# Block-sparse attention with a gated projection on one core: output weights staged in other buffers, projections gated on the value weights alone, new order tables

## The chip, the cores and the metric

One core of a Trainium2 chip runs the whole program in one launch. The metric is device time in microseconds (us) from one execution; lower is better. The engines are TensorE (PE, with its weight loads shown as PEld), VectorE (DVE), ScalarE (ACT), GpSimd (POOL) and SyncE (SP, which here only issues transfers).

## The reference

Attention over 4 batches, 8 heads, 768 positions, head size 64, in blocks of 32. A query block sees its own block and the two beside it, the first and the last block, and three drawn blocks; the first and the last query block see all. The attention output, written as rows of 512, then goes through a gated projection:

```python
scores = np.where(mask, scale * np.matmul(q, k.transpose(0, 1, 3, 2)), -1000000000.0)
attn = softmax(scores)                       # over the seen keys
x = np.matmul(attn, v)                       # -> (4, 768, 512)
for k in range(5):                           # causal convolution along the rows
    gate_pre += conv_w[k][None, None, :] * xp[:, k:k + S, :]
gate = 1.0 / (1.0 + np.exp(-gate_pre))
out = (gate * (x @ w_val)) @ w_out           # w_val, w_out: 512 x 512
```

## The kernel before, in words

The unit of attention work is a pair of neighbouring query blocks (11 pairs in a batch) or half of the first-and-last query blocks (two units in a batch), 52 units in all. The main loop runs one step for each unit n, and in a step it writes, for each engine, the work of several units that are in different states: the scores of unit n (`sc`, or `s` for the first-and-last blocks), the products with the values of unit n-2 (`av`), the turning of the probabilities of unit n-1 (`pt`), and the turning of the attention rows of unit n-3 (`xp`) into `xT`. The other engines serve these: DVE takes the row maxima (`mx`) and normalizes (`rs`, `x`); ACT takes the exponentials (`pe`, or `rest` and `first`), copies the turned probabilities from PSUM (`ptr`), copies `xT` and scales the queries (`qc`); POOL gathers the value rows of drawn blocks by an indirect transfer (`vb`) and copies drawn key blocks (`kg`). Which engine copies which key block, scales the queries of which batch, and so on is set by strings of letters at the head of the file (`KEYS_BY`, `OWN_BY`, `Q_ON`, `NEAR`). Each engine executes its instructions in the order in which they were written.

Beside attention runs the gated projection. A batch's rows are two tiles of 384. For a tile, `gates` makes the gate (ACT `th` and DVE `th`, 16 DVE passes of 128x384), `split` writes `xT` as a rounded part `xh` (four ACT passes) and a rest `xl` (four POOL passes), and `project` multiplies with the value weights (`vp`, 48 matmuls), evicts the gated values (`y`, `yh`, `yl`) and multiplies with the output weights (`op`, 36 matmuls). How many pieces of `project` and of the preparation stand at which half step is set by the digits in `FILLS` and `STEPS`.

The weights arrive as 64-bit words in eight chunks of 512 KB (four of `w_val`, then four of `w_out`), each into a staging buffer `wst`. Four decode passes on DVE (`words`, `wst`, `wst`, `words`), a cast on ACT (`wv` or `wo`) and a subtraction on POOL or DVE turn a chunk into a rounded part and a rest. Before the change all eight chunks are staged in the buffers of `xh`, `xl`, `yh` and `yl`, four at a time, so `split` may begin only when the last four are staged and two of them are decoded, and `project` only when all eight are decoded.

Of the kernel before, what the change touches and what calls it, by code (L numbers as in the profile page):

```python
# [20 lines left out]
DM = H * D  # L21
# [9 lines left out]
V_AT = ((0, 3, 7), (1, 4, 8), (0, 1, 4), (1, 3, 8))  # L31
K_AT = ((9, 10, 11), (11, 11, 11), (2, 11, 11), (1, 4, 4))
LAG_T, LAG_V, LAG_X = 1, 2, 3
WEIGHTS_AT = (0, 1, 6, 7, 8, 10, 12, 15)
# [7 lines left out]
    "PPAAAAPPPAAAPPPAAAPPPAAAPPPAAAPPPAAAPPPAAAPPPAAAPPPAAAPPPAAAPPAAAA",  # L42
    "AAAPPPPAASSSPPPSSSPPPPAAPPPSSSPPPVVVPPPSSSPPPSSSPPPSSSSSSSSSPPPSSS",
    "SSSSSSSSSSSSPSSSSSPPPPPSPPSSSSPPSSSSPSVVVVPSSSSSPPSSSSPSSSSSPSSSSS",
    "PASSSSPASSSSSSAAAAPASSSSAVSSSSPASSSSPASSSSSSSSSAPAASSSVVVVVVPASSSS",
)
NEAR = (
    "GGGGGGCCGGGGGCGCGGGGGG",
    "GGGGGGGGGGGGGGGGGGGGGG",
    "GGGGGGGGGCGGGGGGGGCGGG",  # L50
    "GGGGGGGGGCCGGGGGGGCGCG",
)
Q_ON = "AAVV"
OWN_BY = (
    "DPDPDPDPDVDPDPDPVPDPDP",
    "DPDPDPPPDPDPDPAPPPVPDA",
    "ADADADADADADADAAADADAD",
    "PPPPPPPPDPPPPPPPPVPPPP",
# [4 lines left out]
XT_ON = "VVAAAAAAAAAAAVAAAAAAAAAAVAAAAAAAAAAAAAAAAAAVVAVAVAVA"  # L63
GATHER = "WUGGGGGGGUGSSSSUSUGSGUSGSSGGGSSGGGGGGGGGGGSGGGGGGGGGGUUU"

BULK_BY = "SSSSSASSSSSSSSSASSSSSSSSSSSSSSSS"
# [8 lines left out]
    "11200001313200100202234322"  # L75
    "00020031021101112223041301"
    "21011101111121012110010202"
    "11011021212101010101050101"
    "213030"
)  # L80
STEPS = (
    "20111015213401132202221312"
    "21304021020202020314440534"
    "02311340003240051012082142"
    "23320113212020102130402231"
    "000012"
# [5 lines left out]
def attention_moe(ctx, tc, qb, kb, v, ve, sampled, w_val, conv_w, w_out, ident_in, slot_in, out):  # L92
# [148 lines left out]
    staged = []  # L241

# [4 lines left out]
    def load_weights():  # L247

        for n in range(2 * CH):
            st = const.tile([128, CH, TS], F32R, tag=("xh", "xl", "yh", "yl")[n % 4], name="wst")  # L250
            flat = st.bitcast(I32).rearrange("p c n -> p (c n)")[:, 0 : 2 * DM]
            c = n % CH
            queue(24 + n).dma_start(flat, (w_val if n < CH else w_out).bitcast(I32)[c * 128 : (c + 1) * 128, :])
            staged.append((step[0], flat.rearrange("p (n w) -> p n w", w=2)))
            yield
# [514 lines left out]
    def queue_rows(bt, t):  # L770
        m = Rows()
        m.bt, (m.t, m.n), m.ready, m.begun = bt, TILES[bt.b][t], [], False
# [11 lines left out]
    def fill(times=1):  # L784
        for _ in range(times):
            if set(range(2 * CH)) <= decoded and to_project and step[0] > max(to_project[0][0].ready):
                begun.add("project")
                advance(to_project)
# [168 lines left out]
```

## Time and profile before

| | |
|---|---|
| median of 3 runs | 365.35 us (364.81 to 367.18) |
| the profiled execution, whole | 366.3 us |
| its span, first to last instruction | 364.4 us |
| PE busy | 346.8 us, 95% of the span |
| DVE, ACT, POOL busy | 268.2, 249.4, 219.0 us |
| mean granted TensorE clock | 0.984 |

The profiled execution lies 0.95 us above the median, and 1.9 us of it lie outside the span. In the profile's rows an engine's idle time stands in brackets with what ended it; `[0.66 <-ACT ptr L110]` means that the engine stood for 0.66 us until ACT's write of `ptr`. All instructions go through one recording helper, so their line is L110 in all rows, and they are told apart by their tiles. Times are from the span's start.

### The profile page before, as it was taken

Reading aid. Unit: us, or ns where it says so; the run is one execution under the profiler, and the core shown is the slowest. Engines: PE = TensorE matmul, PEld = TensorE weight load, DVE = VectorE, ACT = ScalarE, POOL = GpSimd, SP = SyncE. Lnnn points to the kernel's source line nnn. Section 1 sums busy time; section 2 is a strip of 40 time slices with the busy share of each in tenths; the row PEclk is TensorE's granted clock in tenths of the full one; section 3 lists DMA queues with packets and bytes.
Section 4 is the critical chain, followed back from the end, with each engine's and each line's share of the span. In section 5 each row is a group of like instructions: output and inputs, shape, how many; then the busy total and the mean of one; then the engine's idle time right before and its main releaser. Section 6 shows DMA issues by size and latency. Waiting matters only on the chain.

```text
span 364.4 us, 14299 instructions
## 1 busy us (share of the span) xinstructions
PE 346.8 (95%) x5650; PEld 273.0 (75%) x5650; DVE 268.2 (74%) x616; ACT 249.4 (68%) x613; POOL 219.0 (60%) x327
## 2 busy tenths in 40 slices
PE   8698999997999999999999999999999999999995
PEld 7265576664676977787689787986798778989894
DVE  3559769978798788885988588966957878485930
ACT  2678799998798576777695776975655867645431
POOL 1775758799885585776653684566537544525440
PEclk9689999999999999999999999999999999999999
DMA  6997996999559985975457289776432244110202
GB/s 218 309 349 209 303 271 207 297 309 290 152 166 310 265 251 160 293 225 151 116 163 246 70 246 269 212 223 205 120 109 89 77 150 147 31 58 31 86 2 87
DMA packets 44644, 68.08 MB, mean 187 GB/s; under 512 B 6081, under 2 KB 26945, under 8 KB 44577
## 3 DMA queue, kind: packets, MB, share of 16 engines
q1 hardware_dynamic: 36704, 43.09, 39.1%
q0 software_dynamic: 6880, 22.77, 20.9%
q10 hardware_dynamic: 992, 1.30, 1.2%
q8 instruction: 45, 0.74, 0.8%
q14 instruction: 23, 0.18, 0.2%
HBM read 60.84 MB, written 6.29 MB: 184 GB/s over the span
## 4 chain that ended last, share of the span: by engine, by line
PE 63%; ACT 5%; DVE 3%; POOL 1%; issue 1%; ACTq 0%; DVEq 0%
PE vp L110 18%; PE op L110 17%; PE av L110 10%; PE pt L110 8%; PE sc L110 7%; PE xp L110 2%; PE s L110 1%; ACT ptr L110 1%; ACT pe L110 1%; DVE qc L110 1%; ACT th L110 1%; POOL yl L110 1%; POOL vb L110 1%; DVE mx L110 1%; ACT ot L110 0%
## 5 line engine op out<-in xcount | busy, mean ns | idle before, releaser
L110 POOL DMA_INDIRECT vb<-in_v,idx x88 | 88.5, 1006 | 71.1 <-PE av L110 46.4
L110 ACT ACTIVATE pe<-sc,mx 128x256 f32<-128x256 f32 x176 | 69.3, 485 | 36.9 <-DVE mx L110 36.7
L110 DVE SCALAR_TENSOR_TENSOR th<-xT,cw,th 128x384 f32<-128x384 f32 x128 | 89.0, 706 | 4.6 <-ACT th L110 2.3
L110 DVE TENSOR_REDUCE mx<-sc 128x2 f32<-128x512 f32 x88 | 56.6, 684 | 24.1 <-PE sc L110 23.9
L110 ACT COPY ptr<-pt 128x512 f32<-128x512 f32 x103 | 59.9, 610 | 4.4 <-PE pt L110 4.3
L110 POOL COPY kg<-k 128x128 f32 (+1 forms) x163 | 56.9, 387 | 9.5 <-DMA k<-in_k 9.1
L110 PE MATMUL sc<-kg,qc 64*32 64x256 f32 x1408 | 57.5, 399 | 5.3 <-POOL kg L110 3.2
L110 POOL TENSOR_TENSOR yl<-y,yh 128x384 fp32r<-128x384 f32 x32 | 32.5, 1021 | 38.6 <-ACT yh L110 36.4
L110 PE MATMUL op<-wo,yh 128*128 128x512 f32 x192 | 53.7, 401 | 0.0
L110 PE MATMUL vp<-xh,wv 128*128 128x384 f32 x256 | 51.4, 343 | 0.0
L110 PE MATMUL pt<-ident,pe 128*128 128x128 f32 x352 | 50.9, 283 | 0.0
L110 PEld LDWEIGHTS av<-va,ptr 128*32 128x32 f32 (+1 forms) x1056 | 30.9, 118 | 24.3 <-ACT ptr L110 13.1
L110 PE MATMUL av<-va,ptr 128*32 128x65 f32 (+1 forms) x1056 | 40.4, 226 | 4.4 <-ACT ptr L110 3.4
L110 PEld LDWEIGHTS vp<-xh,wv 128*128 128x128 f32 x256 | 43.9, 188 | 0.2
L110 PEld LDWEIGHTS pt<-ident,pe 128*128 128x128 f32 x352 | 39.1, 142 | 5.8 <-issue 0.8
L110 PEld LDWEIGHTS sc<-kg,qc 64*32 64x32 f32 x1408 | 24.9, 109 | 24.4 <-issue 8.8
L110 POOL TENSOR_TENSOR xl<-xT,xh 128x384 fp32r<-128x384 f32 x32 | 33.4, 1050 | 11.3 <-ACT xh L110 11.3
L110 PEld LDWEIGHTS op<-wo,yh 128*128 128x128 f32 x192 | 35.0, 188 | 7.0
L110 PE MATMUL av<-vb,ptr 128*32 128x65 f32 x1408 | 38.3, 222 | 1.8 <-DMA vb<-in_v,idx 1.6
L110 PEld LDWEIGHTS av<-vb,ptr 128*32 128x32 f32 x1408 | 30.3, 110 | 4.0 <-DMA vb<-in_v,idx 2.1
L110 PE MATMUL op<-wo,yl 128*128 128x512 f32 x96 | 31.9, 412 | 0.2 <-POOL yl L110 0.2
L110 DVE SCALAR_TENSOR_TENSOR y<-th,vp 128x384 f32<-128x384 f32 x32 | 17.6, 550 | 19.2 <-PE vp L110 16.3
(74 smaller groups left out, 470.9 us busy)
## 6 DMA issues: line engine op xcount, KB each, us to landing
kg<-in_k SPq DMA_DIRECT2D x111, 64.0 KB
qc<-in_q SPq DMA_DIRECT2D x48, 128.0 KB
out<-ot SPq DMA_DIRECT2D x23, 256.0 KB
vn<-in_v SPq DMA_DIRECT2D x11, 520.0 KB
va<-in_v SPq DMA_DIRECT2D x44, 130.0 KB
k<-in_k SPq DMA_DIRECT2D x11, 512.0 KB
wst<-in_w_val SPq DMA_DIRECT2D x4, 512.0 KB
wst<-in_w_out SPq DMA_DIRECT2D x4, 512.0 KB
```

The costliest lines, as they stand in the source:

```text
L110: made = getattr(self.eng, name)(*args, **kwargs)
```

## The change: what it does

The four value chunks stay in the buffers of `xh`, `xl`, `yh` and `yl`. Three of the four output chunks go into one buffer of `xT`, the one that the second batch's turned rows use later, and the fourth into a gate buffer `th`. `split` needs only the first two value chunks to be decoded; `project` needs only the value weights for its first four pieces and all weights for the rest. All the tables at the head of the file are written anew.

```diff
-V_AT = ((0, 3, 7), (1, 4, 8), (0, 1, 4), (1, 3, 8))
-K_AT = ((9, 10, 11), (11, 11, 11), (2, 11, 11), (1, 4, 4))
+V_AT = ((1, 3, 7), (3, 3, 6), (1, 1, 6), (0, 3, 5))
+K_AT = ((9, 11, 11), (11, 11, 11), (3, 9, 10), (1, 3, 4))
-WEIGHTS_AT = (0, 1, 6, 7, 8, 10, 12, 15)
+WEIGHTS_AT = (0, 0, 6, 6, 7, 10, 11, 15)
...
-    "AAAPPPPAASSSPPPSSSPPPPAAPPPSSSPPPVVVPPPSSSPPPSSSPPPSSSSSSSSSPPPSSS",
+    "SSSSAAAAAAAASSSAAAPPPPAAPPPSSSSSSAAAPPPSSSPPPSSSPPPSSSPPPSSSPPPPSS",
...
-Q_ON = "AAVV"
+Q_ON = "AAVA"
...
     staged = []
+    wide_room = two.tile([128, CH, KW - 1 + S], F32, tag="xT", name="wst")
...
         for n in range(2 * CH):
-            st = const.tile([128, CH, TS], F32R, tag=("xh", "xl", "yh", "yl")[n % 4], name="wst")
-            flat = st.bitcast(I32).rearrange("p c n -> p (c n)")[:, 0 : 2 * DM]
+            if n < CH:
+                st = const.tile([128, CH, TS], F32R, tag=("xh", "xl", "yh", "yl")[n], name="wst")
+            elif n == 2 * CH - 1:
+                st = two.tile([128, CH, TS], F32, tag="th", name="wst")
+            else:
+                st = wide_room
+            first = 2 * DM * (n - CH) if CH <= n < 2 * CH - 1 else 0
+            flat = st.bitcast(I32).rearrange("p c n -> p (c n)")[:, first : first + 2 * DM]
...
     def fill(times=1):
         for _ in range(times):
-            if set(range(2 * CH)) <= decoded and to_project and step[0] > max(to_project[0][0].ready):
+            if not to_project or step[0] <= max(to_project[0][0].ready):
+                return
+            m = to_project[0][0]
+            if set(range(CH if m.groups < CH else 2 * CH)) <= decoded:
                 begun.add("project")
+                m.groups += 1
                 advance(to_project)
...
-        if {CH, CH + 1} <= decoded and len(staged) == 2 * CH and to_split and unread <= {id(to_split[0][0])}:
+        if {0, 1} <= decoded and to_split and unread <= {id(to_split[0][0])}:
             advance(to_split, prepared)
...
-        if k < 2 * CH and n >= WEIGHTS_AT[k] and (k < 4 or k - 4 in decoded):
+        if k < 2 * CH and n >= WEIGHTS_AT[k]:
             next(weights)
```

What the tables do shows in the order of the engines' instructions. On PE the first `vp` keeps its place: in both kernels it is row 582 of PE's order, in step 23, and the order of kinds of matmuls around it is the same. What moves is the work of the other engines.

On ACT, in steps 11 and 12 of the loop before the change, from the copies of the turned halves (`ptr`) of step 11 on:

```order
L110 COPY ptr<-pt 128x512 x2
L110 CAST wo_156<-words 128x512
L110 COPY xT<-xp 128x4x64
L110 ACTIVATE qc<-qc 128x256
L110 ACTIVATE pe<-sc,mx 128x256 x4
```

On ACT, in the same place of step 11 now:

```order
L110 COPY ptr<-pt 128x512
L110 CAST xh<-xT 128x384
L110 COPY ptr<-pt 128x512
L110 CAST wo_156<-words 128x512
L110 CAST xh<-xT 128x384
L110 COPY xT<-xp 128x4x64
```

Two of the four `xh` casts of the first tile stand in step 11 now, one of them between the two `ptr` copies; the other two follow in step 12, behind six copies of drawn key blocks (`kg` 128x128) where two stood.

On ACT, in step 15 before the change, where the first two casts stood:

```order
L110 COPY ptr<-pt 128x512
L110 CAST wo_156<-words 128x512
L110 CAST xh<-xT 128x384
L110 COPY ptr<-pt 128x512
L110 CAST xh<-xT 128x384
```

On ACT, in step 15 now:

```order
L110 COPY ptr<-pt 128x512 x2
L110 CAST wo_156<-words 128x512
L110 ACTIVATE th<-xT,cw 128x384
L110 COPY xT<-xp 128x4x64
L110 ACTIVATE qc<-qc 128x256
```

Both turned halves are copied ahead of the cast of the output weights, which stood between them. In step 14 a gate's first pass (`th`) stood between the two copies, and stands in step 15 now; a `wo` cast went from step 13 to step 14.

On POOL, from the value weights' subtraction of step 11 on, now (before, `wv` was followed by the `vb` row at once, the four `xl` stood in steps 15 to 17, and step 12 had one `kg` copy of a drawn block more, step 13 three more):

```order
L110 TENSOR_TENSOR wv_155<-words,wv_154 128x512
L110 TENSOR_TENSOR xl<-xT,xh 128x384
L110 DMA vb<-in_v,idx 128x520 x2
L110 COPY kg_147<-k 128x256
L110 COPY kg_147<-k 128x2x128
L110 TENSOR_TENSOR wo_157<-words,wo_156 128x512
L110 TENSOR_TENSOR xl<-xT,xh 128x384 x2
L110 DMA vb<-in_v,idx 128x520 x2
```

The subtractions `xl`, each of which needs ACT's `xh`, stand ahead of the value gathers `vb` of the next step now.

Further moves: the drawn key blocks of step 10 are one fewer on ACT, those of step 11 one fewer, those of step 13 three more. In step 18 three drawn key blocks went from DVE, where they stood between the row maxima and the decode passes of the last weight chunk, to ACT. The scaling of the fourth batch's queries (`qc`) left DVE for ACT as a whole. The third chunk of output weights is loaded a step earlier; the steps in which the chunks are decoded stay the same but for one.

## Rows read from the trace of the kernel before

**Rows 1.** The page's first part: busy time, share of the span, instructions.

```profile
PE 346.8 (95%) x5650; PEld 273.0 (75%) x5650; DVE 268.2 (74%) x616; ACT 249.4 (68%) x613; POOL 219.0 (60%) x327
```

**Rows 2.** Stretches: length, then busy PE, PEld, DVE, ACT, POOL, clock, DMA.

```profile
60.67:77.22 16.55, 15.73 (x362) 11.43 (x361) 15.39 (x36) 16.05 (x46) 13.29 (x22) 1.00 0.98 289
77.22:119.31 42.09, 37.89 (x783) 27.24 (x783) 34.70 (x85) 35.88 (x90) 33.22 (x58) 1.00 0.79 237
119.31:240.00 120.69, 120.26 (x2074) 97.87 (x2072) 98.40 (x214) 84.12 (x203) 74.81 (x105) 1.00 0.70 206
```

**Rows 3.** The chain that ended last: start, length, what.

```profile
108.66 1.17 PE av L110 x44
...
137.39 1.02 PE sc L110 x32
138.41 1.21 PE av L110 x48
139.62 1.02 PE pt L110 x8
...
142.05 0.22 PE xp L110 x2
```

**Rows 4.** PE in order of time: start, length, what, idle before and its end.

```profile
79.97 0.57 PE L110 MATMUL av<-va,ptr 128*64 128x65 f32 x12 [0.66 <-ACT ptr L110]
...
84.97 0.57 PE L110 MATMUL av<-va,ptr 128*64 128x65 f32 x12 [1.30 <-ACT ptr L110]
...
91.01 0.66 PE L110 MATMUL av<-vb,ptr 128*32 128x65 f32 x30 [1.22 <-DMA vb<-in_v,idx]
...
119.31 1.64 PE L110 MATMUL vp<-xh,wv 128*128 128x384 f32 x8
```

**Rows 5.** ACT in order of time, steps 11, 15 and 18.

```profile
65.16 1.01 ACT L110 COPY kg<-k 128x128 f32 x4
66.07 1.06 ACT L110 COPY ptr<-pt 128x512 f32<-128x512 f32 x2
67.13 0.62 ACT L110 CAST wo<-words 128x512 fp32r<-128x512 f32 x1
67.66 0.36 ACT L110 COPY xT<-xp 128x256 f32<-128x256 f32 x1
...
83.40 0.62 ACT L110 CAST wo<-words 128x512 fp32r<-128x512 f32 x1 [0.96 <-DVE words L110]
83.93 0.51 ACT L110 CAST xh<-xT 128x384 fp32r<-128x384 f32 x1
84.34 0.58 ACT L110 COPY ptr<-pt 128x512 f32<-128x512 f32 x1
...
100.53 0.62 ACT L110 CAST wo<-words 128x512 fp32r<-128x512 f32 x1 [1.39 <-DVE words L110]
```

**Rows 6.** POOL in order of time, steps 13 and 15.

```profile
72.14 0.99 POOL L110 DMA_INDIRECT vb<-in_v,idx  x1 [2.02 <-PE av L110]
...
83.81 0.94 POOL L110 DMA_INDIRECT vb<-in_v,idx  x1 [0.30 <-issue]
...
86.01 0.99 POOL L110 TENSOR_TENSOR xl<-xT,xh 128x384 fp32r<-128x384 f32 x1
```

**Rows 7.** DVE in order of time, step 18.

```profile
97.47 0.29 DVE L110 TENSOR_SCALAR_CACHE_REDUCE kg<-k 128x128 f32 x1 [0.87 <-issue]
...
98.34 0.16 DVE L110 TENSOR_SCALAR rs<-av 128x4 f32<-128x4 f32 x1
```

**Rows 8.** Two scalings of queries on DVE, in order of time.

```profile
259.93 0.29 DVE L110 TENSOR_SCALAR qc<-qc 128x256 f32<-128x256 f32 x1
276.38 4.17 DVE L110 TENSOR_SCALAR qc<-qc 128x256 f32<-128x256 f32 x1
```

**Rows 9.** The stretch around the longer one, columns as in rows 2.

```profile
275.00:280.00 5.00, 5.00 (x96) 3.87 (x94) 4.09 (x2) 2.49 (x6) 5.00 (x7) 1.00 0.34 102
```

**Rows 10.** PE in order of time, behind that stretch.

```profile
284.78 0.34 PE L110 MATMUL av<-va,ptr 128*32 128x65 f32 x8 [0.63 <-ACT ptr L110]
```

More of the change, by code (lines that the diff above doesn't have):

```diff
@@ L41 @@
 KEYS_BY = (
-    "PPAAAAPPPAAAPPPAAAPPPAAAPPPAAAPPPAAAPPPAAAPPPAAAPPPAAAPPPAAAPPAAAA",
-    "AAAPPPPAASSSPPPSSSPPPPAAPPPSSSPPPVVVPPPSSSPPPSSSPPPSSSSSSSSSPPPSSS",
-    "SSSSSSSSSSSSPSSSSSPPPPPSPPSSSSPPSSSSPSVVVVPSSSSSPPSSSSPSSSSSPSSSSS",
-    "PASSSSPASSSSSSAAAAPASSSSAVSSSSPASSSSPASSSSSSSSSAPAASSSVVVVVVPASSSS",
+    "PPAAAAPPPAAAPPPAAAPPPAAAPPPPAAPPPAAAPPPAAAPPPAAAPPPAAAPPPAAAPPPAAA",
+    "SSSSAAAAAAAASSSAAAPPPPAAPPPSSSSSSAAAPPPSSSPPPSSSPPPSSSPPPSSSPPPPSS",
+    "SSSSSSPPSSSSSSSSSSPPPPPSPPPSSSPSSSSSPSVVVVPSSSSSPPSSSSPSSSSSPSSSSS",
+    "PASSSSPASSSSSSAAAAPASSSSAVSSSSPASSSSPASSSSPASSSSPAASSSVVVVVVPASSSS",
 )
 NEAR = (
-    "GGGGGGCCGGGGGCGCGGGGGG",
+    "GGGGGGCCGGGGCCCCGCGCGG",
     "GGGGGGGGGGGGGGGGGGGGGG",
-    "GGGGGGGGGCGGGGGGGGCGGG",
-    "GGGGGGGGGCCGGGGGGGCGCG",
+    "GGCGGGGGGCGGGGGGGGCGGG",
+    "GGGGGGGGGGGGGGGGGGCGCG",
 )
-Q_ON = "AAVV"
+Q_ON = "AAVA"
 OWN_BY = (
     "DPDPDPDPDVDPDPDPVPDPDP",
-    "DPDPDPPPDPDPDPAPPPVPDA",
-    "ADADADADADADADAAADADAD",
-    "PPPPPPPPDPPPPPPPPVPPPP",
+    "DPDPDPPPDPDPDPAPPPDPDA",
+    "VDADADADADADADAAADADAD",
+    "PPPPPPDPPPPPPPPPPVPPPP",
 )
@@ L62 @@
 PTR_ON = "AAAAAAAAAVAAAAAAAAAAAAAVAAAAAAAAAAAAAAAAAAAAAVAVAVAAAAAAAAAAAAAAAAAAAAVAVAAAAAAAAAAVAAVAAAAAAAAAAAAAAAAA"
-XT_ON = "VVAAAAAAAAAAAVAAAAAAAAAAVAAAAAAAAAAAAAAAAAAVVAVAVAVA"
-GATHER = "WUGGGGGGGUGSSSSUSUGSGUSGSSGGGSSGGGGGGGGGGGSGGGGGGGGGGUUU"
-BULK_BY = "SSSSSASSSSSSSSSASSSSSSSSSSSSSSSS"
+XT_ON = "VVAAAAAAAAAAAVAAAAAAAAAAAAAAAAAAAAAAAAAAAAAVVAVAVAVA"
+GATHER = "WUGGGGGGGUGSSSSUSUGSGUSGSSGGGSSGGGGGGGGGGGSGGGWGGGGGGGGG"
+BULK_BY = "SSSASASSSSSSSSSASSSSSSSSSSSSSSSS"
 Q_BY = "SSSS"
@@ L74 @@
 FILLS = (
-    "11200001313200100202234322"
-    "00020031021101112223041301"
+    "21000211202000011202214303"
+    "12200200201020111334041301"
     "21011101111121012110010202"
-    "11011021212101010101050101"
-    "213030"
+    "11011021231101010101040101"
+    "210003"
 )
 STEPS = (
[L82 to L86, printed above, removed]
+    "20111015213433102202220411"
+    "21030521020202023014440543"
+    "02311340003240051109002142"
+    "23320103002200211140522121"
+    "001002"
 )
@@ L771, in queue_rows @@
         m = Rows()
-        m.bt, (m.t, m.n), m.ready, m.begun = bt, TILES[bt.b][t], [], False
+        m.bt, (m.t, m.n), m.ready, m.begun, m.groups = bt, TILES[bt.b][t], [], False, 0
         to_gate.append((m, gates(m)))
```

## The prediction

> **What bounds the kernel now.** I read the page's first part, then the stretches, then the chain that ended last, then each engine in order of time around the places where the chain leaves PE. PE is busy for 95% of the span [rows 1], so whatever the change does, it can give back only time in which PE stands or its products are stretched. The stretches show where that is. Behind the first projection, which starts at 119.31 us [rows 4], PE is busy for 120.26 of the next 120.69 us [rows 2]; projections fill the gaps there, and the chain runs through PE from piece to piece. Ahead of it there are only attention steps, and the chain runs through ACT and DVE until 108.66 us, where it enters PE and stays [rows 3]. An attention step at PE's own pace costs 1.02 + 1.21 + 1.02 + 0.22 = 3.47 us [rows 3]. The stretch of the four steps 11 to 14 takes 16.55 us [rows 2] where 4 x 3.47 = 13.9 would do, and ACT is busy for 16.05 us of it, 97%: ACT is the bound there. In the stretch behind it, steps 15 to 22 and the start of 23, ACT is busy for 35.88 of 42.09 us and PE for 37.89 [rows 2]; there single waits bind: products with values stand 0.66 and 1.30 us for `ptr` from ACT and 1.22 us for gathered rows [rows 4].
>
> **What the change doesn't do.** It lets projections begin with the value weights alone, but the first `vp` keeps its place in PE's order, step 23, behind the same attention work. So no PE work is added, removed or carried into the empty first third. What counts is how early step 23 is reached, which each step ahead of it decides one to one, since the chain is PE from 108.66 us on, and then the small losses behind it.
>
> **Part by part, steps 0 to 10.** One key copy fewer on ACT in step 10: 1.01 us for four in time and 0.91 us to the next instruction [rows 5], so 0.23 us each. I count it below. The bulk loads of the second batch's keys come in other steps, two copies of near value rows go to DVE: I set them at nothing; without a gap beside it an added copy on DVE would delay a row maximum by about its own length, and the nearest row, a key copy, has 0.29 us [rows 7], so +0.6 for the two at most, and -0.6 if the moved loads give as much back.
>
> **Steps 11 to 13: more on ACT.** An `xh` cast occupies ACT for 84.34 - 83.93 = 0.41 us, a `wo` cast for 67.66 - 67.13 = 0.53 us [rows 5]. Step 10 loses one key copy (-0.23); step 11 gains two casts and loses a copy (0.82 - 0.23 = +0.59); step 12 gains two casts and four copies (0.82 + 0.92 = +1.74); step 13 gains three copies and loses a `wo` cast (0.69 - 0.53 = +0.16). The sum is +2.26. Since ACT is busy 97% of this time it lies on the path, except for the 0.5 us in which ACT stands [rows 2]: bounds +1.8 and +2.3. I take **+2.3**, because ACT's few idle moments come from waits which remain.
>
> **Steps 14 to 16: waits that go.** In step 14 a gate's first pass stood between the two `ptr` copies, in step 15 a `wo` cast that itself stood 0.96 us for DVE's decode, and an `xh` cast [rows 5]; the second copy was late by that, and PE stood 0.66 and 1.30 us for it [rows 4]. In the new order both copies come first. Who is late next? The exponentials behind the cast, and the gathered rows. Four casts (-1.64) leave ACT in steps 15 and 16, a `wo` cast comes to step 14 (+0.53), so ACT has room for the exponentials. I take **-2.0**, the two waits. The third wait, 1.22 us for gathered rows, has bounds on both sides: gone (-1.2), or longer (see the second rival). The four `xl` no longer stand on POOL ahead of or between these gathers, which helps, but they, and with them the gathers of steps 12 and 13, are later in the steps before, which hurts. The gather which PE awaited left POOL at 83.81 + 0.94 = 84.75 us [rows 6] and its rows were there at 91.01 us [rows 4], so 6.26 us of transfer that POOL's order doesn't shorten. I take 0 for it.
>
> **Step 18.** Three key copies leave DVE. With the wait ahead of them they hold it from 97.47 - 0.87 = 96.60 to 98.34 us [rows 7], 1.74 us, just ahead of the decode passes for which ACT's `wo` cast stands 1.39 us until 100.53 us [rows 5]. But ACT makes the copies now: it would come to the cast at 100.53 - 1.39 + 0.69 = 99.83 us instead of 99.14, with the decoded words there 1.74 us earlier than before. The cast moves by 100.53 - 99.83 = **-0.7**. Lower bound -1.4 (all of the wait), upper bound 0, if the new copies delay `ptr`.
>
> **Behind 119 us.** The queries' scaling of the last batch goes from DVE to ACT. A scaling takes 0.29 us on DVE, but one took 4.17 us [rows 8], in a stretch in which POOL was busy for 5.00 of 5.00 us [rows 9]; the row maxima behind it were late, then the exponentials, then `ptr`, and PE stood 0.63 us at 284.78 [rows 10]. That wait goes: **-0.6**. ACT gets a pass per step in return, and it has room, with 84.12 us busy of 120.69 in the long stretch before [rows 2]; without room each pass would cost at most its own length. The other tables move single copies under PE's cover: 0, bounds of half a microsecond either way. The tail, from the last scores on, has the same order on PE.
>
> The Trainium skill, page "SBUF — State Buffer", section "SBUF: two separate sides", states that DVE in a two-port mode and POOL take a shared pair of ports as an exclusive lock, so that the later one stands for the whole instruction. The rows of the 4.17 us pass agree as far as they go: DVE was held while POOL worked without a pause [rows 8, 9]. By that rule the change is right to take scalings from DVE, and wrong to put four `xl` passes of POOL beside the decode passes and copies of DVE in steps 11 to 13; this is the third rival.
>
> **The sum.** 2.3 - 2.0 - 0.7 - 0.6 = -1.0 us against the profiled execution: 366.3 - 1.0 = 365.3. That execution stood 0.95 us above the median of 365.35, so for a median the forecast is 365.35 - 1.0 = 364.35, say **364.3 us**.
>
> **Rivals.** *First, the steps behind 15 run at PE's pace.* If the earlier split takes all pressure from steps 15 to 22, PE's whole idle time there, 42.09 - 37.89 = 4.2 us [rows 2], goes in place of my 2.7, and if PE's own stretched products in steps 11 to 14 hide the new work on ACT, the +2.3 falls away too: -4.2 - 0.6 = -4.8, or 360.5 us. With only the first half it is -2.5, 362.8. For it: the waits of [rows 4] end on ACT or on gathers, which the split stood beside. Against it: 97% of ACT in the steps before.
>
> *Second, slower: POOL's queue.* In its order `xl` of step 11 stands ahead of the gathers of step 12 and needs `xh`, which ACT now makes behind a `ptr` copy, so POOL stands until about 67 us (ACT copies `ptr` from 66.07 us [rows 5]) and the gathers start late; the two `xl` of step 12 do the same to the gathers and key copies of step 13. An `xl` holds POOL for about 0.99 us [rows 6]; four are 4 us, plus the waits for `xh`; POOL has one reserve there, 2.02 us of idle ahead of 72.14 [rows 6], and 3.26 us idle in all of the 16.55 [rows 2], and loses four key copies. The four passes less that reserve are 1.94 us, some 2.5 with the waits for `xh`; if the gather that left POOL at 84.75 so leaves at 87.3, its rows come 6.26 us later, at 93.6, where PE met them at 91.01: +2.6, on top of ACT's +2.3, with the 2.0 swallowed by this wait, -0.7 and -0.6 kept: 2.6 + 2.3 - 1.3 = +3.6, or 369.0 us at the worst. It decides from the point at which that gather leaves POOL more than some 2 us later than PE itself is shifted. For it: DMA is 98% busy in steps 11 to 14 [rows 2]. Against it: the reserve, and PE's own shift of 2.3 us hides as much lateness.
>
> *Third, DVE is held by POOL.* DVE is busy for 15.39 of 16.55 us in steps 11 to 14 [rows 2]. A decode pass, a copy of value rows or a gate pass that meets one of the four `xl` stands up to 0.99 us; all four would make DVE's work 15.39 + 3.96 = 19.35 us, 0.5 us more than the 16.55 + 2.3 = 18.85 that ACT makes of the stretch; with DVE's own idle 1.16 us kept as well it is 1.7 us more. That gives 364.8 to 366.0 us, no change.
>
> **How the numbers follow.** The forecast has 0.43, the first rival 0.25, the second 0.17, the third 0.15. A measurement of this kernel tells about 1%, 3.7 us, from no change. Faster by over 1%, under 361.7 us, holds in most of the first rival's cases and a few of the forecast's: 0.20. Slower by over 1%, over 369.0 us, holds in the second rival's worst cases: 0.11. The rest, 0.69, lies between. The range runs from the first rival's 360.5 to just short of the second's worst, 368.5.
>
> **What would show it.** The first `vp` tells the sum of all steps ahead of it: I expect it near 118.9 us (2.3 - 2.0 - 0.7 = -0.4). The scores of step 15, at 77.2 us before (the bound between the stretches), should start near 79.5; if earlier, my ACT term is too big, if later than 80.5 with POOL's gathers or `kg` as the wait's end, the second rival holds. No wait for `ptr` should be left near 80 and 85 us; in step 18 the `wo` cast's wait should be short; no scaling should be long behind 240 us. The prediction is wrong if the projections ahead of 130 us find PE waiting for `yh` or `yl`, or if ACT, with the last batch's scalings, makes PE stand in the stretch from 240 to 300 us.

## The result, and the profile after

The changed kernel takes 368.53 us, the median of 22 runs (367.28 to 369.95), the kernel before in the same runs 366.06 us (22 runs, 364.12 to 373.26). The ratio is 1.0055 with a 95% interval of 1.0034 to 1.0075: slower by half a per cent. It leaves out the executions of a second, slower state; the medians of all runs alone would give 1.0067. The forecast of 364.3 us was 4.2 us too low, and the time lies just over the upper end of its range (368.5). The experiments below were timed in five groups, each with its own measurement of the kernel before, 366 to 367 us in the third and fourth and 376 to 379 us in the others, whose traces carry additional stalls of unknown cause. Ratios are taken within a group. Traces of the one kind are not set against those of the other, but for one step behind 280 us, and it is said there why.

The profiled execution of the changed kernel took 367.28 us, its span is 365.5 us (before 366.3 and 364.4). First the page's first part, to be read against [rows 1]: the same work on PE, 5.6 us more on ACT, 3 us more on POOL.

```profile
PE 348.3 (95%) x5650; PEld 273.2 (75%) x5650; DVE 269.7 (74%) x600; ACT 255.0 (70%) x633; POOL 222.0 (61%) x325
```

Then the stretches, cut at the same scores as [rows 2] (steps 11 to 14, steps 15 to 22 with the start of 23, the 120.69 us behind the first projection); columns as there.

```profile
58.81:80.50 21.69, 17.55 (x361) 11.79 (x361) 20.45 (x37) 17.80 (x52) 16.75 (x20) 0.92 0.83 234
80.50:121.75 41.25, 39.11 (x784) 26.86 (x783) 37.03 (x80) 35.74 (x91) 30.03 (x54) 1.00 0.77 232
121.75:242.44 120.69, 120.58 (x2076) 98.36 (x2075) 100.39 (x214) 85.81 (x208) 76.61 (x105) 1.00 0.71 208
```

Read as a ledger, after less before: up to the scores of step 11 -1.86 us (58.81 against 60.67); steps 11 to 14 **+5.14** (21.69 against 16.55); steps 15 to 22 -0.84 (41.25 against 42.09); behind the first `vp` -1.34 (365.5 - 121.75 = 243.75 against 364.4 - 119.31 = 245.09). The sum is the +1.1 of the spans. The first entry is mostly this execution, the fastest of the 22: three variants of the changed kernel, profiled later, reach step 11 at 59.92, 59.97 and 61.69 us. Without it the change costs 2.96 us by the traces, and 2.0 us by the ratio.

The whole loss stands in four steps, and there the busiest engine is no longer ACT (16.05 of 16.55 us before [rows 2], now 17.80 of 21.69) but DVE, 20.45 of 21.69. DVE in order of time, step 13:

```profile
68.48 0.42 DVE L110 TENSOR_SCALAR words<-wst 128x512 f32<-128x512 f32 x1
68.81 3.85 DVE L110 TENSOR_SCALAR row<-base 128x24 f32<-128x24 f32 x1
72.70 0.18 DVE L110 TENSOR_TENSOR row<-row,valid 128x24 f32<-128x24 f32 x1
72.92 0.18 DVE L110 TENSOR_SCALAR idx<-row 128x24 int32<-128x24 f32 x1
73.13 0.42 DVE L110 COPY vb<-va 32x520 f32<-32x520 f32 x1
73.58 1.29 DVE L110 TENSOR_REDUCE mx<-sc 128x2 f32<-128x512 f32 x2
```

A pass of 24 columns took 3.85 us, where the 512 columns ahead of it took 0.42. POOL in the same stretch:

```profile
68.49 1.00 POOL L110 COPY kg<-k 128x256 f32<-128x256 f32 x2
69.46 1.26 POOL L110 TENSOR_TENSOR wo<-words,wo 128x512 fp32r<-128x512 f32 x1
70.69 1.93 POOL L110 TENSOR_TENSOR xl<-xT,xh 128x384 fp32r<-128x384 f32 x2
73.86 0.99 POOL L110 DMA_INDIRECT vb<-in_v,idx  x1 [1.24 <-issue]
```

Five passes without a gap, from 68.49 to 72.62 us; DVE's pass ends at 72.66. Before, POOL stood for 2.02 us ahead of the gather at 72.14 [rows 6]; the two `xl` fill that gap now. What the held pass did further down, PE and then ACT in order of time:

```profile
70.31 0.69 PE L110 MATMUL av<-va,ptr 128*64 128x65 f32 x16 [0.88 <-ACT ptr L110]
...
73.61 0.66 PE L110 MATMUL av<-vb,ptr 128*32 128x65 f32 x30 [2.38 <-DVE vb L110]
```

```profile
74.31 1.57 ACT L110 ACTIVATE pe<-sc,mx 128x256 f32<-128x256 f32 x4 [2.14 <-DVE vb L110]
```

Behind `row` in DVE's queue stand the copy `vb` that PE needs and the maxima `mx` that ACT needs, so both stood. The chain that ended last has the pass as a piece of its own (start, length, what):

```profile
68.90 3.78 DVE row L110
```

The copy `vb` of step 13 is itself new. The kernel before copies near value rows on DVE at 57.48 and 62.09 us and then not again ahead of the first `vp`; the changed kernel has one more in step 12 and the one of step 13 that PE waits for:

```profile
64.78 0.42 DVE L110 COPY vb<-va 32x520 f32<-32x520 f32 x1
```

For some 3 us behind the hold PE also worked at the lower of its two clock levels (0.50 of full speed; columns as in [rows 2]), so that the two `xp` products of step 13 took 0.63 us where they take 0.38 in the other steps:

```profile
75.00:78.00 3.00, 3.00 (x39) 1.45 (x39) 2.90 (x5) 3.00 (x11) 2.84 (x4) 0.50 0.72 193
```

What was expected behind it did come. The waits of [rows 4] are gone but for 0.15 us, as these rows of PE show; so is the wait of the `wo` cast in step 18 (1.39 us in [rows 5]), as the row of ACT shows:

```profile
82.85 0.57 PE L110 MATMUL av<-va,ptr 128*64 128x65 f32 x12 [0.15 <-ACT ptr L110]
...
86.44 0.69 PE L110 MATMUL av<-va,ptr 128*64 128x65 f32 x16
...
91.77 0.67 PE L110 MATMUL av<-vb,ptr 128*32 128x65 f32 x32
...
121.75 0.42 PE L110 MATMUL vp<-xh,wv 128*128 128x384 f32 x1
```

```profile
102.08 0.64 ACT L110 CAST wo<-words 128x512 fp32r<-128x512 f32 x1
```

### The profile page after: what moved, and what is told of

Read it like the earlier page. It is cut to its first block, busy times and chain, and to the rows that moved or that the text cites. A ratio compares the mean times of both kernels' runs of the same rounds, so it can differ in the third digit from the quotient of the medians.

```text
span 365.5 us, 14296 instructions
## 1 busy us (share of the span) xinstructions
PE 348.3 (95%) x5650; PEld 273.2 (75%) x5650; DVE 269.7 (74%) x600; ACT 255.0 (70%) x633; POOL 222.0 (61%) x325
## 4 chain that ended last, share of the span: by engine, by line
PE 70%; DVE 12%; ACT 7%; issue 3%; POOL 3%; DMA 2%; ACTq 1%; POOLq 1%; SPq 0%; DVEq 0%
PE vp L110 18%; PE op L110 17%; PE av L110 12%; PE pt L110 10%; PE sc L110 8%; DVE mx L110 4%; PE s L110 2%; ACT ptr L110 2%; DVE th L110 2%; PE xp L110 2%; DMA k<-in_k 2%; ACT pe L110 1%; DVE rest L110 1%; POOL kg L110 1%; POOL vb L110 1%
## 5 line engine op out<-in xcount | busy, mean ns | idle before, releaser
L110 DVE SCALAR_TENSOR_TENSOR th<-xT,cw,th 128x384 f32<-128x384 f32 x128 | 91.5, 725 | 4.4 <-ACT th L110 2.0
L110 POOL COPY kg<-k 128x128 f32 (+1 forms) x161 | 59.0, 405 | 8.4 <-DVE early L110 6.4
L110 POOL TENSOR_TENSOR yl<-y,yh 128x384 fp32r<-128x384 f32 x32 | 33.4, 1045 | 38.7 <-ACT yh L110 36.4
```

What stands on the lines that cost most here:

```text
L110: made = getattr(self.eng, name)(*args, **kwargs)
```

## Experiments

**Theory A**: DVE's passes between SBUF tiles are held while POOL works without a pause, and the early `xl` made such a pause-free run at a bad place. **Theory B**: ACT's added work lengthens steps 11 to 14. **Theory C**: the `row` pass is slow for a reason of its own. **A2**, in later expectations, is a narrower form of A: the hold lasts over several POOL passes only where POOL's next pass does not wait for earlier work of POOL.

### Undoing one thing at a time (first group)

The changed kernel itself was not timed in this group; its 1.0055 comes from the measurement above.

The split as late as before, all else as changed:

```diff
-        if {0, 1} <= decoded and to_split and unread <= {id(to_split[0][0])}:
+        if {CH, CH + 1} <= decoded and len(staged) == 2 * CH and to_split and unread <= {id(to_split[0][0])}:
```

> The changed kernel with the old condition for split, so that the four xh casts and xl passes of the first tile stand in steps 15 to 17 again; staging, tables and the rest as changed. Theory A (the small DVE passes of step 13 were held off by POOL's unbroken run of two key copies, wo and two xl, 68.5 to 72.6 us): the interval from the scores of unit 13 to those of unit 14 falls from 8.3 us to 4 to 4.5; waits for ptr and gathers of 1 to 2 us come back in steps 15 to 17; in all 2 to 3 us faster than the changed kernel, about 366. Theory B (the added work of ACT in steps 11 to 13, 2.3 us): the interval falls by about 2 us, and the whole by 1 us or less, since the work only moves to steps 15 and 16.

Measured: 0.9869 (0.9798 to 0.9939). The loss is gone, and more than the loss. Step 13, from its scores to those of step 14, takes 6.53 us in this trace with additional stalls; A had expected 4 to 4.5.

The low half of the first `wo` chunk on DVE, which parts POOL's run:

```diff
-LOW_ON = "PVPPPPPP"
+LOW_ON = "PVPPVPPP"
...
-                if LOW_ON[n] == "V":
+                if LOW_ON[n] == "V" and n < CH:
```

> The changed kernel with one subtraction moved: the rest of the first output chunk (wo, step 12) on DVE in place of POOL. ACT's order is the same to the last instruction. POOL's run in step 12 then has a gap between the key copies and the two xl, which wait for ACT's xh. Theory A: the row pass of step 13 takes under 1.2 us in place of 3.85, the interval of step 13 falls by 3 us or more, the whole to about 365.5, in spite of 0.7 us more on DVE. Theory B: no change beyond 0.7 us, 368 to 369.

Measured: 1.0081 (1.0032 to 1.0130), no gain. A's time is missed. The `row` pass takes 0.17 us in its trace, but DVE has a subtraction more, its pass ahead of `row` is held instead, beside one `xl`, and PE still waits 1.35 us for `vb`. That pass on DVE:

```profile
79.97 1.26 DVE L110 TENSOR_SCALAR words<-wst 128x512 f32<-128x512 f32 x1
```

The three row passes of the second batch made earlier, in the first batch's fourth pair; then that, and one near copy of step 13 gathered instead of copied (one `C` of `NEAR` to `G`):

```diff
-        if pr.p == 0 and b:
+        if (b, pr.p) == (0, 4):
+            indices(1)
+        if pr.p == 0 and b > 1:
             indices(b)
```

> The changed kernel with the three small DVE passes that make the second batch's row numbers (row, row, idx) written in step 4 in place of step 13; POOL's run and the copy of near value rows behind these passes stay. Theory A: the copy of near rows (0.42 us) is now the pass that is held, to about 72.6 us plus its own length, so PE's wait for it stays at about 2 us and the whole falls by only 0.5 to 1 us, to about 367.7. Theory C (the row pass was slow for a reason of its own, as a wait for the gathers that read the numbers): the wait goes as a whole, 364.5.

And with the copy gone as well:

> As e3_rows_early, and the copy of near value rows of step 13 is replaced by gathering 128 rows in place of 96, as the kernel before has it. Nothing of DVE that uses SBUF on both sides is left in that place but a decode pass ahead of POOL's run. Theory A: PE's wait of 2.4 us goes, the interval of step 13 falls from 8.3 to about 4.5 us, the whole to about 364.8, under the kernel before. Theory B: about 368 (the ACT work is still there). Theory C: the same as e3.

Measured: 1.0062 (1.0012 to 1.0111) and 1.0008 (0.9966 to 1.0050). DVE, POOL and then PE in order of time, rows early, show why the first gained nothing:

```profile
80.42 2.11 DVE L110 TENSOR_SCALAR words<-wst 128x512 f32<-128x512 f32 x1
82.56 0.42 DVE L110 COPY vb<-va 32x520 f32<-32x520 f32 x1
```

```profile
80.30 1.94 POOL L110 TENSOR_TENSOR xl<-xT,xh 128x384 fp32r<-128x384 f32 x2
```

```profile
83.04 0.66 PE L110 MATMUL av<-vb,ptr 128*32 128x65 f32 x30 [1.68 <-DVE vb L110]
```

With `row` out of the way the next pass of DVE, `words` (0.42 us alone), meets POOL's two `xl` and stands. Theory C falls. With the copy gone as well PE no longer waits for `vb`, but `words` is held as long (2.12 us), the row maxima come late and PE stands 1.14 us for them; so A's gain came only in part, and without the changed kernel in the group the times can't say how much.

### The xl alone (second and fourth group)

The changed kernel once more, as a measure; and with ACT's casts left early and only POOL's four `xl` held back until the first output chunks are decoded. ACT's order is the same to the last row.

```diff
             if c:
+                held.append(c - 1)
+            while held:
+                if not {CH, CH + 1} <= decoded:
...
+                h = held.pop(0)
                 pool.tensor_tensor(
...
```

Of the changed kernel itself:

> The changed kernel unaltered, as the measure for the runs beside it. All theories: its time stands to the kernel before as 1.0055 (368.5 to 366.1 us). Its trace shows whether the 3.85 us row pass of DVE and the 8.28 us from the scores of step 13 to those of step 14 come back in another execution. Theory A (DVE's pass is held while POOL works without a pause): yes, 3 to 4 us, wherever the pass meets POOL's run. If the pass takes 0.2 us here and the interval is near 4 us, the first trace showed an accident.

With `xl` late, and once more in the fourth group:

> The changed kernel with the four early casts of xh left on ACT in steps 11 to 13, and only POOL's four xl subtractions moved behind the first two output chunks, where they were before. ACT's order is that of the changed kernel to the last row. Theory A (POOL's unbroken run with the xl passes holds DVE's small row pass): the run falls apart, the row pass takes 0.2 us, and step 13 (from its scores to those of step 14) falls from 8.3 to 4 to 5 us; the kernel gains 2 to 4 us on the changed one, ratio to the kernel before 0.995 to 1.000. Theory B (ACT's added casts lengthen steps 11 to 13): nothing is given back, 1.005 and step 13 stays at 8 us. Theory C (the row pass is slow for a reason of its own): it stays at 3 to 4 us although POOL's run is broken.

> The changed kernel with only POOL's four xl moved late once more, among quieter executions. Theory A: 0.993 to 1.000, step 13 (from its scores to those of step 14) 4 to 5 us, no wait of PE for vb over 1 us. Theory B: 1.003 to 1.007, step 13 as long as in the changed kernel.

Measured: the changed kernel 1.0014 (0.9980 to 1.0049); `xl` late 0.9948 (0.9911 to 0.9985) beside it, and 0.9994 (0.9958 to 1.0030) in the fourth group. The changed kernel's own 1.0014 lies under the 1.0055 expected: in this group its loss can't be told from nothing, while `xl` late gains 0.66% on it, 2.5 us. In its second trace the hold is there again, shorter than the 3 to 4 us expected and this time on `words`; DVE, POOL and PE:

```profile
77.55 2.19 DVE L110 TENSOR_SCALAR words<-wst 128x512 f32<-128x512 f32 x1
```

```profile
77.50 1.95 POOL L110 TENSOR_TENSOR xl<-xT,xh 128x384 fp32r<-128x384 f32 x2
```

```profile
80.76 0.43 PE L110 MATMUL av<-vb,ptr 128*32 128x65 f32 x16 [2.27 <-DVE vb L110]
```

With `xl` late (fourth group) the `row` pass takes 0.17 us, and PE waits for DVE's `vb` once, for 0.2 us. DVE's pass, and steps 11 to 14 there:

```profile
69.72 0.17 DVE L110 TENSOR_SCALAR row<-base 128x24 f32<-128x24 f32 x1
```

```profile
59.92:79.00 19.08, 16.64 (x361) 11.17 (x360) 16.75 (x41) 18.58 (x57) 14.43 (x21) 1.00 0.96 275
```

That is 2.61 us less than in the changed kernel and still 2.53 more than before, and ACT is busy for 18.58 of 19.08 us. Step 13 takes 5.30 us, where A expected 4 to 5, against 8.28 in the changed kernel and 3.95 before. Both theories have their part: A the 2.6, and B, as far as ACT's share tells, the 2.5; the late split below takes these 2.5 further apart.

### POOL's passes one by one (third and fourth group)

Each compute pass of POOL waits until the one before it is complete, which parts every run without moving a pass: in the changed kernel, with the late split, and in the kernel before.

```diff
+                    both = self.eng is nc.gpsimd and "dma" not in name and "dma" not in self.name
+                    kind = mybir.DependencyClass.Sync if both else mybir.DependencyClass.NoSync
                     tc.add_manual_dep(
                         made.ins, self.last.name,
-                        mybir.DependencyInfo(mybir.DependencyClass.NoSync, mybir.DependencyReason.DATA),
+                        mybir.DependencyInfo(kind, mybir.DependencyReason.DATA),
...
```

In the changed kernel:

> The changed kernel with the same work in the same order on PE, DVE and POOL; only each compute pass of POOL behind another now waits until that one is complete. Theory A2: POOL's run of two copies, wo and two xl in steps 12 and 13 no longer holds DVE from end to end; a small pass of DVE that meets it is held 1.2 us at most, PE's wait of 2.3 to 2.4 us for vb falls under 1 us, and the kernel comes 1 to 3 us under the changed one, ratio to the kernel before 0.994 to 1.000. Theory B (ACT's casts) and theory C (the row pass by itself): no gain, 1.001 to 1.006. A cost of its own, some hundredths of a us for each wait on POOL, would show as idle time of POOL, of which there is enough behind step 16.

With the late split:

> The changed kernel with the split as late as before and POOL's passes one by one: both remedies at once. Theory A2: the best of all, the late split took 0.987 by itself (interval 0.980 to 0.994), so 0.985 to 0.993. Theory B: the late split alone does it, and the waits add nothing or cost a little: 0.987 to 0.995.

In the kernel before:

> The kernel before with nothing changed but that POOL's compute passes wait for one another. Theory A2: its one long scaling (4.17 us near 276 us) lasts 1.2 us at most, the stretch behind gains about 1 us without moving any work to ACT, ratio 0.995 to 0.999. Otherwise 1.000 to 1.003.

Measured: 1.0174 (1.0121 to 1.0228), 1.0182 (1.0133 to 1.0230), 1.0274 (1.0212 to 1.0335), all misses on the time. The hold does break: in the first the worst pass of step 13 is `idx`, held about 1 us, and in the third the scaling that took 4.17 us [rows 8] takes 0.74 (DVE in each):

```profile
75.20 1.13 DVE L110 TENSOR_SCALAR idx<-row 128x24 int32<-128x24 f32 x1
```

```profile
287.17 0.74 DVE L110 TENSOR_SCALAR qc<-qc 128x256 f32<-128x256 f32 x1
```

But the waits are not cheap on POOL. The list of waits of the kernel before, one by one (what waited for what: us in total, times, longest), first POOL's, then PE's:

```profile
POOL kg L110 <- POOL kg L110: 11.3, 22, 1.0
```

```profile
PE av L110 <- DMA vb<-in_v,idx: 6.2, 4, 2.1
PE sc L110 <- POOL kg L110: 5.9, 5, 2.2
```

Its key copies wait up to 1.0 us for one another, and PE stands for late keys and gathered rows. So the wait belongs only where the run does harm: on the low halves of the weights and the first tile's `xl`, some eight of them.

```diff
+                out=lo, in0=t.bitcast(F32), in1=hi.bitcast(F32), op=ALU.subtract, alone=not on_dve
...
-                    op=ALU.subtract,
+                    op=ALU.subtract, alone=m.bt.b == 0 and m.t == 0,
```

> The changed kernel, the same order on every engine; only the low halves of the weights (wv, wo) and the first tile's four xl wait until POOL's pass before them is complete, some eight waits instead of the two hundred of the last run with POOL one by one, which broke the long hold (1.13 us at most) and yet lost 1.7% since POOL's copies and gathers came late. Theory A2: the pass of 3.85 us takes 1.3 us at most, PE's wait of 2.38 us for vb falls under 1 us, and 1.5 to 3 us of the changed kernel's time go: ratio to the kernel before 0.995 to 1.001. Theory B (ACT's casts): no gain, 1.003 to 1.007.

Measured: 1.0020 (0.9992 to 1.0048), between what A2 (up to 1.001) and B (from 1.003) expected; its interval overlaps that of the changed kernel, so the time alone shows no gain. DVE in order of time, and steps 11 to 14 with the stretch behind:

```profile
69.98 0.37 DVE L110 TENSOR_SCALAR row<-base 128x24 f32<-128x24 f32 x1
...
70.94 1.39 DVE L110 COPY vb<-va 32x520 f32<-32x520 f32 x1
```

```profile
59.97:79.05 19.08, 16.87 (x362) 11.28 (x361) 17.55 (x41) 18.44 (x56) 15.21 (x19) 1.00 0.90 255
...
79.05:120.50 41.45, 38.12 (x783) 27.07 (x783) 36.10 (x77) 34.85 (x88) 30.48 (x55) 1.00 0.81 240
```

The longest hold in step 13 is 0.97 us (1.39 less 0.42), PE waits for DVE's `vb` once, for 0.2 us, and the four steps take 19.08 us, to the hundredth what they took with `xl` late: two different ways of parting DVE from POOL's run end on the same ACT.

### The late split again, and the late term (fourth, second and fifth group)

The late split:

> The changed kernel with the split as late as before once more, since its first measurement fell among executions of 372 to 382 us. Theory A: the hold in step 13 is gone, the gains of staging elsewhere, of step 18 and of the queries on ACT stay: 0.992 to 0.998. Rival: the first ratio (0.987) was a matter of those executions, 0.998 to 1.003.

Measured: 0.9926 (0.9893 to 0.9960), 364.25 us against 366.65 in its group. This version beats both kernels, the changed one by 1.3% if the ratios of the two measurements are divided (0.9926 / 1.0055). Its steps, without the casts of `xh` on ACT, in the same two stretches:

```profile
61.69:79.89 18.20, 15.81 (x361) 11.24 (x361) 16.36 (x41) 17.19 (x53) 14.14 (x21) 1.00 0.96 278
...
79.89:120.23 40.34, 38.23 (x784) 27.34 (x783) 35.74 (x77) 36.23 (x92) 31.77 (x52) 1.00 0.83 242
```

What PE waits for `ptr` in the second of these stretches (us in total, times, longest):

```profile
PE av L110 <- ACT ptr L110: 0.6, 2, 0.3
```

Set against the changed kernel this is the price of the early split by itself: from step 11 to the first `vp` it takes 58.54 us against 62.94. With the casts early and only `xl` late it is 61.11, so the casts alone cost 2.57 us, as the times say (0.9994 less 0.9926, 0.7%, 2.5 us). Only 0.88 us of that lie in steps 11 to 14 (19.08 against 18.20); the rest lies behind them, where PE stands 0.9 us for gathered rows. And of the 2.53 us that steps 11 to 14 are longer than before, 1.65 are there without the early casts too. The changed kernel's other work for ACT in these steps, the added copies of key blocks, is the nearest cause; no run takes it out by itself.

Where the 2.4 us come from that the late split gains on the kernel before, the one trace tells only in part: steps 11 to 22 take 58.54 us against 58.64 before, and behind the first `vp` it has 244.5 against 245.1.

The fourth batch's queries alone, first put on ACT in the kernel before, then put back on DVE in the late split:

```diff
-Q_ON = "AAVV"
+Q_ON = "AAVA"
```

On ACT in the kernel before:

> The kernel before with one letter changed: the fourth batch's queries are scaled on ACT. It measures the late term by itself. My term: -0.6 us; the offset between the traces behind 284 us says -1.1 us. So 0.997 to 0.998 of the kernel before, and no scaling longer than 0.5 us behind 240 us. Rival: ACT has no room, each of the scalings costs its length of some 0.3 us on the path, and the ratio is 1.000 to 1.003.

On DVE in the late split:

> The changed kernel with the split as late as before (0.993 of the kernel before) and the fourth batch's queries scaled on DVE again, as before. It undoes my late term of -0.6 us by itself. If the late term is what the offset between the traces says, -1.1 us, the ratio goes from 0.993 to 0.996, a scaling over 3 us long comes back near 277 us, and PE waits behind it. Rival: with other work beside it no long scaling comes back, and the ratio stays at 0.991 to 0.994.

Measured: 0.9998 (0.9957 to 1.0040) and 0.9914 (0.9862 to 0.9965); neither interval can tell 1.1 us from nothing. The traces can: from one set of scores to the next PE takes 5.86 us where [rows 10] has its wait, and 4.74 with the queries on ACT. PE in order of time, the kernel before, then it with the queries on ACT:

```profile
282.41 1.09 PE L110 MATMUL sc<-kg,qc 64*32 64x256 f32 x32
...
288.27 1.09 PE L110 MATMUL sc<-kg,qc 64*32 64x256 f32 x32
```

```profile
291.56 1.09 PE L110 MATMUL sc<-kg,qc 64*32 64x256 f32 x32
...
296.30 1.09 PE L110 MATMUL sc<-kg,qc 64*32 64x256 f32 x32
```

The last two kernels belong to groups with additional stalls, but behind 280 us the steps agree: the next one takes 4.74 us in all three. In the kernel before with POOL's passes one by one, where the scaling takes 0.74 us on the same DVE, the step takes 4.73.

But with the queries on DVE again, in the late split, it is 4.73 as well, and no pass is held for more than 1.4 us; DVE's longest scalings there:

```profile
265.35 1.67 DVE L110 TENSOR_SCALAR qc<-qc 128x256 f32<-128x256 f32 x1
...
285.77 1.63 DVE L110 TENSOR_SCALAR qc<-qc 128x256 f32<-128x256 f32 x1
```

So the 1.1 us is the price of one meeting of a scaling with POOL's run. Moving the scaling avoids it, and so did the changed tables without that; the rival of this run holds.

### The hold by itself (probes)

Four kernels of their own, which leave out the computation: POOL makes runs of passes, DVE beside it two or three small ones. The core of the first:

```python
for n, w in enumerate(run):
...
    if w == "s":
        pool.tensor_tensor(out=last, in0=a, in1=b, op=ALU.subtract)
...
dve.tensor_reduce(out=mx, in_=psum, axis=AX.X, op=ALU.max)
for n in range(2):
    form(kind, const.tile([128, 24], F32, name=f"d{n}_{tag}"))
```

Of the first:

> A kernel of its own that leaves out all of the computation and writes zeros: DVE reduces a PSUM bank, then makes two small passes of one form (128x24, about 0.2 us each alone) while POOL makes no pass, one, two or five subtractions of 128x384, five copies of 128x256, or two and three subtractions with a wait for ACT between them. Theory A: beside five passes a held form takes as long as the rest of POOL's run, 3 to 4 us, and the second one 0.2 us; with the wait in between it ends at the wait, at 1 to 2 us; forms that are not held take 0.2 us throughout. Narrow rule (held for one POOL instruction at most): no pass is longer than 1.2 us, and with five passes both may be held, one after the other. Theory C: all small passes take 0.2 us beside any run.

Of the second, in which POOL's passes differ in what they wait for:

> A second kernel of its own that leaves out all of the computation and writes zeros. As in the first probe DVE makes two small passes while POOL works, but POOL's passes now differ in what they wait for: three or five passes that wait for nothing (sss, sssss, kkkkk for copies), passes into tiles used before, which wait for an earlier pass of POOL that is long complete (ooooo), passes that each read the one before (ccccc), and passes that each wait for a finished pass of ACT (aaaaa). Theory A2 (DVE gets the ports at a boundary only where POOL's next pass waits on POOL's own completion): beside sssss, kkkkk and aaaaa the first held pass lasts until POOL's whole run ends, about 4 us, 1.5 us for kkkkk; beside ccccc, and ooooo, at most 1.0 us, as in the first probe. Narrow rule (at most one POOL instruction): never more than 1.0 us beside any run. If sssss holds for 4 us and ooooo too, it is the dependence on the pass just before that opens the ports.

Of the third, with the types and the loads of the kernel:

> A third kernel of its own that leaves out all of the computation and writes zeros, nearer to the place in the kernel: five POOL subtractions of 128x384 (s plain, f written as fp32r from an fp32r operand as xl is, w the same with each pass waiting for a finished pass of ACT), DVE passes of 128x24 (ts), 128x512 (wd) and 128x512 from two operands (st), first in a quiet machine (q), then with loads of 1.5 MB each under way (l). In the first two probes a pass was held for one POOL pass at most (0.71 us), in the kernel for four (3.85 us). Theory A2 in its narrow form: the hold over several passes needs what the kernel has and the first probes had not, so one of f, w or l shows a pass of more than 1.5 us. If none does, what makes the hold last over several passes stays open, and only that it does is shown.

Of the fourth, the place itself:

> A fourth kernel of its own that leaves out all of the computation and writes zeros. It builds the place of the long hold: POOL's two copies of 128x256, a subtraction of 128x512 written as fp32r (wo) and two of 128x384 (xl) without a wait of POOL on itself, and on DVE three small passes row of 128x24, behind nothing (r) or behind a 128x512 pass from every second word (w), started at three delays, with ACT and PE idle (i) or at work (b). If what lets the hold last is the neighbourhood (the shapes, the pass ahead of it, ACT and PE at work), one row takes over 1.5 us in some of the twelve cases. If every row takes under 1.3 us, as in the three probes before, the cause of the long hold is in something that these probes don't have, and stays open.

Single tiles' rows (instructions; shortest, median, longest in ns; when): two from the first probe beside five POOL passes, one from the second beside passes with an operand per row, one from the third and one from the fourth:

```profile
L110 DVE TENSOR_SCALAR d_ts_sssss<-a x2: 165/436/706, 31.0 to 31.6; 128x24 f32<-128x24 f32 x2
```

```profile
L110 DVE COPY d_ps_sssss<-psum x2: 173/173/173, 51.8 to 51.9; 128x24 f32<-128x24 f32 x2
```

```profile
L110 DVE TENSOR_SCALAR d_ts_aaaaa<-a x2: 165/240/316, 98.0 to 98.2; 128x24 f32<-128x24 f32 x2
```

```profile
L110 DVE TENSOR_SCALAR d_wd_w_l<-big x2: 961/1086/1212, 99.5 to 100.4; 128x512 f32<-128x512 f32 x2
```

```profile
L110 DVE TENSOR_SCALAR row_iw_256x<-b x3: 166/367/1239, 29.6 to 30.0; 128x24 f32<-128x24 f32 x3
```

The 3 to 4 us that A and A2 expected came in none of them. Beside POOL's subtractions a DVE pass from SBUF to SBUF (one operand, two, or a copy) is held until the POOL pass under way ends, and then gets in, though POOL goes on without a gap: 0.7 to 0.8 us for 0.17 beside one pass, two or five, 1.24 beside the longer `wo`, and 0.96 and 1.21 for two passes of 512 columns. Once, in the second probe, two passes were held one after the other (0.71 and 1.02 us). Beside POOL passes with an operand per row, 1.24 us each, the longest DVE pass took 0.32 us, so not every POOL pass holds DVE to its end. A copy out of PSUM or a reduction of 24 columns is never held (0.17).

The Trainium skill, page "SBUF — State Buffer", section "SBUF: two separate sides", says that of a VectorE pass in a two-port mode, or with two SBUF inputs, and a GpSimd pass whoever starts first has the shared ports for the whole instruction. The probes agree with it to the pass, but for those passes with an operand per row. The kernel's own traces do not: 3.85 us over the ends of four POOL passes, 2.19 us over that of one, 4.17 us with POOL busy throughout [rows 8, 9].

Neither waits of POOL on itself, nor the fp32r output, nor loads under way brought a hold over several passes about. The fourth probe says less than it was built for: in five of its six cases with ACT and PE at work the small passes came ahead of POOL's run or inside its last pass, and the sixth met only its first copy (0.38 us). So the surroundings of the kernel are hardly tested. What lets the hold last in the kernel **stays open**; that it needs POOL's run, and ends with it, is shown.

## Why the prediction was wrong, point by point

**ACT's added work, +2.3.** Right in the total: with the hold away, by either means, steps 11 to 14 take 19.08 us against 16.55, +2.53, and ACT is busy for 97% of them. Its make-up is not confirmed. The sum had 1.64 us for the four casts and 0.62 for the rest; the late split, without the casts, still has 18.20, so by these single traces the casts make 0.88 and the rest 1.65.

**DVE held by POOL, the third rival.** This is the step that failed. It was priced as "up to 0.99 us" for each `xl`, as load on DVE, to be compared with ACT's load, of which only the larger would count: 0.5 to 1.7 us. The load came out near (19.35 us worked out, 20.45 measured), but by luck: the working had four passes held for one `xl` each, and the trace has one pass held over four ends of POOL passes. What was wrong is the comparison, and with it the sum, which has nothing for the hold. The hold fell ahead of `row`, `idx`, `vb` and `mx` in DVE's queue; PE waits for the third of these and ACT for the fourth, and ACT stood for 2.14 us. The copy `vb` was missed too: the prediction counts two new copies of near value rows, both ahead of step 11 and at nothing, and not the two in steps 12 and 13. The two costs add up: 2.5 + 2.6, where the forecast had 2.3 in all. [Rows 6, 8] had shown both halves beforehand: POOL's pause of 2.02 us in step 13, and a pass held for 4.17 us where POOL has no pause. The question that was not asked is which pass of DVE stands in that pause, and who waits behind it.

**Waits in steps 14 to 16 and 18, -2.7 together.** They did go: PE's idle time in the stretch falls from 4.20 to 2.14 us. But the stretch gains only 0.84 us, since PE is busy for 39.11 us against 37.89 with the same products. The 32 `s` products alone cover 4.8 us where they covered 3.2, at the same mean of 0.50 us each: they overlap less, and all the time that any of them covers counts as busy; what kept them apart was not looked into. With few waits on POOL PE is busy for 38.12 us there and idle for more. The term was three times too big because a named wait was taken off the sum whole. Nor was the early split needed for it, which the term gave as its reason ("four casts leave ACT"): in the late split the casts are back behind step 14, PE waits 0.6 us for `ptr` and the stretch takes 40.34 us, less than the 41.25 with the early split.

**The gather of step 15, 0.** Right, and right to set the second rival aside: no wait for gathered rows is left among PE's waits in that stretch, though the four `xl` stand ahead in POOL's queue. That the measured 368.53 us lies so near this rival's 369.0 is chance; what happened is the third rival's hold.

**The late term, -0.6.** Real in the traces, 1.1 us at that place; the 1.34 behind the first `vp` are all that changed there, and 0.6 in the late split, which has the queries on ACT too. The times tell neither from nothing. Its cause, a scaling held by POOL, was right, and moving the scaling to ACT is not the only thing that ends it.

**The first rival,** steps behind 15 at PE's pace: no; the products stayed stretched.

**The signs.** The first `vp` came at 121.75 us, not near 118.9, and the scores of step 15 at 80.50, not 79.5, though this execution reached step 11 early. The waits for `ptr` near 80 and 85 us, that of the `wo` cast and the long scaling behind 240 us went as forecast. One reading was wrong without harm: the chain that ended last does not stay in PE from 108.66 us on, since it has 0.85 us of ACT at 111.11 us and leaves PE again behind 119.

The sum by what was measured: 2.5 + 2.6 - 0.8 - 1.3 = +3.0 us by the traces, where the ratio says +2.0 with an interval of 1.2 to 2.7; the rest is in the steps ahead of 11 and in what single traces can't tell. The working before had -1.0. Of the 4 us between the two workings 2.6 are the hold, 1.9 the waits' over-size and 0.2 ACT's term, less 0.7 from the late term.

## What to carry to other kernels

Moving work to POOL is not free because POOL has idle time: ask which small DVE pass from SBUF to SBUF falls into that idle time now, and what stands behind it in DVE's queue. A hold on one engine and load on another add up if the second waits for something queued behind the held pass; take the larger of the two only when nothing crosses. And of a wait that goes, count what the stretch as a whole can give back, since products that are kept apart still look busy.

## What the runs showed that was not expected

- A hold of DVE over several POOL passes (3.85, 4.17, 2.19 us) exists in the kernel and in none of four probes, the last of which hardly reached the place it was built for.
- Making POOL's passes wait for one another costs 1.7 to 2.7%; some eight such waits at the right place cost nothing that the times show (1.0020, interval 0.9992 to 1.0048, beside 1.0055).
- After PE had stood for 0.88 and 2.38 us in step 13 the granted clock was 0.50 from 75 to 78 us, the lower of its two levels (1.2 and 2.4 GHz), and 0.92 in the mean over steps 11 to 14. It does not go with the hold in every trace: the changed kernel's second trace, with the hold of 2.19 us, has 1.00 in these steps, and the late split with the queries on DVE, without a long hold there, 0.92.
- The early start of the split, which the change makes possible, is what costs: the changed kernel with the split as late as before is faster than both kernels.
